# Two-layer MLP after attention on one core: gate and value products rearranged by Strassen's scheme

## Chip, cores and metric

One core of a Trainium2 chip runs the whole program. The metric is device microseconds (us) of one execution, lower is better. The kernel before took 1002.4, 1003.11 and 1007.12 us in three runs (median 1003.11).

## What is computed

From `q`, `k`, `v` (4 batches, 8 heads, 576 positions, 64 wide) an attention output is the sum of a pooled part (means over 4 positions, softmax, repeated) and a local part (each position sees those less than 4 away). With heads side by side it gives 2304 tokens of 512 values, and two MLPs follow, all in float32:

```
x = x.reshape(2304, 512)
h = x @ moe_w_in                      # 512 x 2048
x = (h - tanh(h)) @ moe_w_out         # 2048 x 512
gate = 1 / (1 + exp(-(x @ moe2_w_gate)))   # 512 x 1536
val = x @ moe2_w_val                  # 512 x 1536
out = (gate * val) @ moe2_w_out       # 1536 x 512
```

## The kernel before

Activations are kept transposed: 128 features in the partitions, tokens along the row. Tokens come in six chunks of N = 384. To get float32 accuracy out of TensorE, every operand is held as a high and a low half in the type float32r, and each product of two 128-wide blocks is three matmuls, high by high, high by low, low by high (`mm3`, L228 to L231). A split costs one ScalarE copy (L239, which writes the high half) and one VectorE subtraction (L224, or L242 where the two are staged apart).

**Stage one** (attention and first MLP). Chunk by chunk the loop runs over 16 column blocks f: `do_h` multiplies a chunk by one 512 x 128 block of `w_in` (12 matmuls into one PSUM bank of the tag ab), ScalarE takes tanh (L554), VectorE subtracts, the result is split to `g`; two blocks later `do_y` multiplies g by a 128 x 512 block of `w_out` (12 matmuls, three into each of four banks acc0 to acc3, which hold the sum over all f). The 16 units of first-layer weights stay in SBUF from chunk 0 on, 14 in the pool `wpa` and 2 in `wpb`. Attention for later chunks is woven in between. At a chunk's end `y_out` (L588) copies the four banks out and stores them to DRAM (`y1`); the last chunk is split straight from PSUM.

**Time in the program is counted in ticks**: each `do_h` and each `do_y` calls `tick` twice, so a tick stands for six matmuls of TensorE, and `defer` and `chain` place VectorE, ScalarE and DMA work so many ticks later. From chunk 1 on ScalarE, VectorE, GpSimd and the DMA queue of SyncE (SP) run in exactly the order in which the program issues their work (`in_order`, L602), so an instruction that waits holds up all behind it on its engine.

**Weights** arrive as 1 MB units of packed 64-bit words (`w_load`, L154). A unit is turned into float32 and split by L170 (ScalarE), L176 and L178 (VectorE), L239 (ScalarE) and L193 (VectorE). Units of the second MLP follow when attention is done and its SBUF is given back (`work`, L678), into slots that the last chunk's first-layer weights leave.

**Stage two** (second MLP). The chunks go in pairs; for each pair the loop runs over 12 column blocks f and the two chunks s. Each step multiplies a chunk by one block of `w_gate` (12 matmuls of 384 columns), ScalarE takes the sigmoid from PSUM (L781), then 12 matmuls for the value, VectorE multiplies (L785), the product is split, and `do_out` of the step before adds g times a block of `w_out` to three banks (9 matmuls of 512 columns). There are 72 steps. At f = 11 the banks are copied out and stored (L765, L757):

```
        gate = a_bank()
        h_mm(weight(2, f, 0), key, gate)
        nc.scalar.activation(out=p, in_=gate[:, :N], func=ACTF.Sigmoid)
        tick()
        val = a_bank()
        h_mm(weight(2, f, 1), key, val)
        nc.vector.tensor_tensor(out=p, in0=val[:, :N], in1=p, op=ALU.mult)
        split(g, p)
```

## Time and profile before

| | us |
|---|---|
| three runs | 1002.4, 1003.11, 1007.12 (median 1003.11) |
| profiled execution, first to last instruction | 998.4 |
| around that span, to the median of the runs | 4.7 |
| TensorE busy (matmul) | 979.2, 98% of the span |
| VectorE busy | 419.2, 42% |
| ScalarE busy | 372.2, 37% |
| GpSimd busy | 78.5, 8% |
| TensorE in the chain that ended last | 91% of the span |

The device time of the profiled execution itself is not listed apart from the three runs, so its span is set against their median. Matmuls are pipelined: a row gives some 0.34 us for a matmul of 384 columns, while the next one starts 0.17 us later. Costs of TensorE are therefore read as spacings between starts, not as durations. On VectorE and ScalarE, too, a queued instruction starts some 0.1 us before the row of the one ahead ends.

### The profile page before, as it was taken

How to read it: one execution, taken by the hardware profiler on the slowest of the kernel's cores; microseconds unless marked ns; L12 is line 12 of the kernel's file. 1: busy time of each engine (PE TensorE's matmuls, PEld its weight loads, DVE VectorE, ACT ScalarE, POOL GpSimd, SP SyncE). 2: the span in 40 equal slices, each digit the busy share in tenths (PEclk: the TensorE clock that was granted, in tenths of full speed). 3: DMA queues.
4: the chain of work that ended last, by engine and by line, in shares of the span. 5: the costliest groups of instructions: out<-in, count | busy, mean ns of one | idle time of the engine just before them, and what ended most of it. 6: DMA issues, size and time to landing. Idle time of an engine off the chain costs nothing.

```text
span 998.4 us, 15616 instructions
## 1 busy us (share of the span) xinstructions
PE 979.2 (98%) x6476; PEld 914.6 (92%) x6476; DVE 419.2 (42%) x736; ACT 372.2 (37%) x952; POOL 78.5 (8%) x89
## 2 busy tenths in 40 slices
PE   7889999999999999999999999999999999999998
PEld 7678889999999889999999999999999999999997
DVE  6898864334334343435666553113211114211112
ACT  5867754344344444434456342113111113111111
POOL 2153220300300320000000000000000000000000
PEclk9899999999999999999999999999999999999999
DMA  8566532212203211104444330002000002000001
GB/s 281 165 216 230 177 113 84 62 40 86 61 9 116 63 61 55 60 1 166 159 142 143 127 127 1 9 16 72 32 1 1 3 22 72 32 1 1 1 1 64
DMA packets 33256, 76.63 MB, mean 77 GB/s; under 512 B 3280, under 2 KB 23456, under 8 KB 28832
## 3 DMA queue, kind: packets, MB, share of 16 engines
q1 hardware_dynamic: 33184, 75.62, 23.0%
q8 instruction: 51, 0.84, 0.3%
q14 instruction: 21, 0.17, 0.1%
HBM read 63.02 MB, written 12.58 MB: 76 GB/s over the span
## 4 chain that ended last, share of the span: by engine, by line
PE 91%; DVE 3%; POOL 2%; DMA 2%; ACT 2%; issue 1%; SPq 0%; POOLq 0%; DVEq 0%; ACTq 0%
PE ab L229 18%; PE ab L231 18%; PE ab L230 18%; PE acc L229 10%; PE acc L230 9%; PE acc L231 9%; PE ab L440 2%; PE ab L372 2%; PE ab L305 1%; PE ab L432 1%; PE ab L346 1%; PE ab L334 1%; DMA qk<-in_qk 1%; DVE w L193 1%; PE acc L653 1%
## 5 line engine op out<-in xcount | busy, mean ns | idle before, releaser
L229 PE MATMUL ab<-x,w 128*128 128x384 f32 x952 | 325.5, 342 | 0.3 <-DVE t L242 0.3
L231 PE MATMUL ab<-x,w 128*128 128x384 f32 x952 | 320.4, 337 | 0.0
L230 PE MATMUL ab<-x,w 128*128 128x384 f32 x952 | 320.1, 336 | 0.0
L229 PEld LDWEIGHTS ab<-x,w 128*128 128x128 f32 x952 | 179.2, 188 | 7.6 <-issue 1.8
L230 PEld LDWEIGHTS ab<-x,w 128*128 128x128 f32 x952 | 179.4, 188 | 3.4
L231 PEld LDWEIGHTS ab<-x,w 128*128 128x128 f32 x952 | 179.2, 188 | 0.0
L785 DVE TENSOR_TENSOR p<-ab,p 128x384 f32<-128x384 f32 x72 | 40.2, 558 | 273.4 <-PE ab L231 273.4
L229 PE MATMUL acc<-g,w 128*128 128x384 f32 x384 | 133.2, 349 | 0.0
L230 PE MATMUL acc<-g,w 128*128 128x384 f32 x384 | 129.7, 338 | 0.0
L231 PE MATMUL acc<-g,w 128*128 128x384 f32 x384 | 129.1, 336 | 0.0
L242 DVE TENSOR_TENSOR t<-ab,t 128x384 f32<-128x384 f32 x94 | 52.3, 556 | 153.4 <-ACT t L554 153.4
L781 ACT ACTIVATE p<-ab 128x384 f32<-128x384 f32 x72 | 35.4, 491 | 183.4 <-PE ab L231 183.4
L554 ACT ACTIVATE t<-ab 128x384 f32<-128x384 f32 x94 | 45.9, 488 | 146.3 <-PE ab L231 130.5
L239 ACT ACTIVATE g<-p 128x384 fp32r<-128x384 f32 x72 | 37.8, 524 | 158.0 <-DVE p L785 158.0
L229 PEld LDWEIGHTS acc<-g,w 128*128 128x128 f32 x384 | 72.1, 188 | 2.4 <-issue 1.8
L230 PEld LDWEIGHTS acc<-g,w 128*128 128x128 f32 x384 | 72.3, 188 | 0.7 <-issue 0.6
L231 PEld LDWEIGHTS acc<-g,w 128*128 128x128 f32 x384 | 72.2, 188 | 0.0
L242 DVE TENSOR_TENSOR g<-t,g 128x384 fp32r<-128x384 f32 x96 | 55.9, 583 | 36.6 <-ACT g L239 35.4
L239 ACT ACTIVATE g<-t 128x384 fp32r<-128x384 f32 x96 | 50.3, 524 | 44.7 <-DVE t L242 44.7
L224 DVE TENSOR_TENSOR g<-p,g 128x384 fp32r<-128x384 f32 x72 | 40.2, 559 | 42.6 <-ACT g L239 42.6
L231 PE MATMUL acc<-w,g 128*128 128x512 f32 x144 | 57.1, 396 | 0.0
L230 PE MATMUL acc<-w,g 128*128 128x512 f32 x144 | 57.0, 396 | 0.0
(101 smaller groups left out, 1099.5 us busy)
## 6 DMA issues: line engine op xcount, KB each, us to landing
raw<-in_w SPq DMA_DIRECT2D x34, 1024.0 KB
qk<-in_qk SPq DMA_DIRECT2D x16, 576.0 KB
vr<-in_vp SPq DMA_DIRECT2D x16, 288.0 KB
x<-xo SPq DMA_DIRECT2D x20, 192.0 KB
xs<-x SPq DMA_DIRECT2D x20, 192.0 KB
y<-y SPq DMA_DIRECT2D x20, 192.0 KB
xs<-y SPq DMA_DIRECT2D x20, 192.0 KB
out<-o SPq DMA_DIRECT2D x12, 256.0 KB
```

The costliest lines, as they stand in the source:

```text
L193: nc.vector.tensor_tensor(out=t[:, 1, :], in0=w32, in1=t[:, 0, :].bitcast(F32), op=ALU.subtract)
L224: nc.vector.tensor_tensor(out=dst[:, 1, :], in0=src, in1=dst[:, 0, :].bitcast(F32), op=ALU.subtract)
L229: nc.tensor.matmul(out=o, lhsT=wh, rhs=xh, start=first, stop=False)
L230: nc.tensor.matmul(out=o, lhsT=wh, rhs=xl, start=False, stop=False)
L231: nc.tensor.matmul(out=o, lhsT=wl, rhs=xh, start=False, stop=last)
L239: nc.scalar.activation(out=dst, in_=src, func=ACTF.Copy)
L242: nc.vector.tensor_tensor(out=dst, in0=a, in1=b, op=ALU.subtract)
L372: nc.tensor.matmul(out=sb[r0:r0 + 64, x, :], lhsT=t[r0:r0 + 64, 0, QB * j:QB * j + QB], rhs=t[r0:r0 + 64, 1, w0:w0 + WIN], start=True, sto ...
L440: nc.tensor.matmul(out=ob[r0:r0 + 64, QB * x:QB * x + QB], lhsT=vw[0][:, j - n, i, r0:r0 + 64], rhs=pt[:, x, r0:r0 + 64], start=True, stop ...
L554: nc.scalar.activation(out=t, in_=hb[:, :N], func=ACTF.Tanh)
L781: nc.scalar.activation(out=p, in_=gate[:, :N], func=ACTF.Sigmoid)
L785: nc.vector.tensor_tensor(out=p, in0=val[:, :N], in1=p, op=ALU.mult)
```

## The change

Stage two is taken apart into a gate-and-value stage and an output stage.

The gate-and-value stage works on a pair of column blocks (j, six of them), a pair of token chunks (p, three) and a side (0 gate, 1 value). The 512 inputs are two halves of two 128-blocks (k and k + 2), so weights and tokens form 2 x 2 blocks, and Strassen's scheme (in the Winograd form) gives the four results from seven products in place of eight. The list `PRODUCTS` names for each the weight form, the token form and the bank. A product is six matmuls (two k, three each); the last three are added onto banks that already hold one of the first four, after that one has been read. `ends_of` is what ScalarE and VectorE do after each product; side 0 uses the four ab banks, side 1 the four acc banks. The results of gate times value go to DRAM (`ud`).

Loops: j outermost, then p, then side. So all token forms (42 tiles: three pairs, two k, seven roles) must be in SBUF at once; they take the space of the first layer's weights as the last chunk finishes with it (`x_room`, `room_free`). Weight forms have one tile per side, refilled for each j. Both are made by three generators (`second_weights` for each side, `forms_of_x`) that run as lanes: after every tick `lanes_step` lets them issue work worth `rate` credits; the numbers that they yield are charged. GpSimd forms the token differences.

The output stage then reads the products back chunk by chunk (`u_load`, four steps ahead), splits them (`u_split`, two steps ahead) and runs the same 72 `do_out` steps back to back, with output weights in slots that the token forms of the first pairs have left. TensorE is issued in program order too from the gate stage on. The last chunk of the first MLP goes through DRAM like the others. First-layer weights are allocated two units to a block. On the host, gate and value weights are put into the order of the 2 x 2 blocks.

The diff, cut to what the prediction speaks of (removed lines of stage two are those quoted above and the loop around them):

```diff
-PAIRS = [(0, LAST), (1, 2), (3, 4)]
+PAIRS = [(0, 1), (2, 3), (4, 5)]
 
 WU = 1024
-U1, U2 = F1, F2 * 3 * 512 // WU
+U1 = F1
+NJ = F2 // 2
+
+A11, A12, A22, S1, S2, S3, S4 = range(7)
+B11, B21, B22, T1, T2, T3, T4 = range(7)
+PRODUCTS = [(A11, B11, 0), (S1, T1, 1), (S3, T3, 2), (A12, B21, 3), (S2, T2, 0), (S4, B22, 1), (A22, T4, 2)]
...
-    n_a, n_b, n_c = 14, 2, 2
-    wpa = pool("wpa", n_a, side="right")
+    n_a, n_b = 14, 2
+    wpa = pool("wpa", n_a // 2, side="right")
...
-    y1 = [dram.tile([128, KD, N], F32, name=f"y_{c}") for c in range(LAST)]
+    y1 = [dram.tile([128, KD, N], F32, name=f"y_{c}") for c in range(NC)]
+    ud = [dram.tile([128, F2, 2, N], F32, name=f"u_{p}") for p in range(len(PAIRS))]
...
+    lanes, credit, rate = [], [0.0], [0.0]
+
+    def lanes_step():
+
+        credit[0] = min(credit[0] + rate[0], 1.5)
+        busy = True
+        while lanes and credit[0] > 0 and busy:
+            busy = False
+            for lane in list(lanes):
+                if lane[1] is not None and not lane[1]():
+                    continue
+                lane[1] = None
+                got = next(lane[0], None)
+                if got is None:
+                    lanes.remove(lane)
+                elif callable(got):
+                    lane[1] = got
+                else:
+                    credit[0] -= got
+                busy = True
+                if credit[0] <= 0:
+                    break
+
+    def lane(g):
+        lanes.append([g, None])
+
+    def after(n):
+        at = now[0] + n
+        return lambda: now[0] >= at
...
-        if c == LAST:
-            x_split1(acc[c][e][:, :N], (2, c), e)
-            return
...
+        if c == LAST:
+            defer(1, stored.add, e)
...
-        if "c" not in wpools and not any(x_left[1:]):
+        if "f" not in wpools and not any(x_left[1:]):
             p1.close()
-            wpools["c"] = pool("wpc", n_c, reuse_waits="tile")
+            wpools["f"] = pool("wpf", 1, reuse_waits="tile")
             wpools["raw2"] = pool("raw2", 1, reuse_waits="tile")
-            wpools["xp2"] = pool("xp2", KD, reuse_waits="tile")
-            w_load(U1 + 2)
+            wpools["xs"] = pool("xs2", 3, reuse_waits="tile")
+            lane(second_weights(0))
+            lane(second_weights(1))
+            lane(forms_of_x())
+            rate[0] = 0.6
...
+    def second_weights(side):
+
+        while len(wt) < U1:
+            yield after(1)
+        for j in range(NJ):
+            raw = raw_load(side, 2 * j + side)
+            yield after(6)
+            yield from to_f32(raw)
+            w, t = (x.bitcast(F32).rearrange("p (b c) -> p b c", b=4) for x in words_of(raw))
+            for o, a, b, op in (
+                (0, w[:, 0], w[:, 3], ALU.add), (2, w[:, 1], w[:, 0], ALU.subtract),
+                (1, t[:, 0], w[:, 1], ALU.subtract), (3, w[:, 2], t[:, 1], ALU.subtract),
+            ):
+                nc.vector.tensor_tensor(out=t[:, o], in0=a, in1=b, op=op)
+                yield 0.45
+            yield lambda: j == 0 or (j - 1, side) in made
+            f = wpools["f"].tile([128, 2, 7, 256], F32R, tag=f"f{side}", name="f")
+            parts = ((w[:, 1:4], slice(0, 3)), (t, slice(3, 7)))
+            for src, at in parts:
+                copy(f[:, 0, at], src)
+                yield 0.0
+            for src, at in parts:
+                nc.vector.tensor_tensor(out=f[:, 1, at], in0=src, in1=f[:, 0, at].bitcast(F32), op=ALU.subtract)
+                yield 1.1
+            form[j, side] = f
+        for i in range(side, NJ, 2):
+            raw = raw_load(side, 2 * NJ + i)
+            yield after(6)
+            yield from to_f32(raw)
+            yield lambda: (NJ - 1, 1, i // 4) in made
+            w32 = words_of(raw)[0].bitcast(F32)
+            t = out_slot(i)
+            copy(t[:, 0, :], w32)
+            yield 0.0
+            nc.vector.tensor_tensor(out=t[:, 1, :], in0=w32, in1=t[:, 0, :].bitcast(F32), op=ALU.subtract)
+            yield 1.3
+            wo[i] = t
...
+            if k < n_a // 2 + 1:
+                t = block(wpa if k < n_a // 2 else wpools["b"], "x").rearrange("p a b -> p (a b)")
+                extra.extend(t[:, 768 * i:768 * i + 768].rearrange("p (i n) -> p i n", i=2) for i in range(5))
+            else:
+                extra.append(xp.tile([128, 2, N], F32R, tag="x", name="x"))
...
+        k = n_blocks[0]
+        return (LAST, min(2 * k + 1, F1 - 1)) in y_done
...
+    def forms_of_x():
+
+        for p, (ca, cb) in enumerate(PAIRS):
+            for k in range(2):
+                yield lambda: room_free()
+                if cb == LAST:
+                    yield lambda: k in stored and k + 2 in stored
+                    yield after(1)
+                raw = {}
+                for n, (c, kk) in enumerate(((cb, k + 2), (cb, k), (ca, k), (ca, k + 2))):
+                    raw[c, kk] = (wpools["xs"] if n < 2 else xs).tile([128, N], F32, tag="xs", name="xs")
+                    nc.sync.dma_start(out=raw[c, kk], in_=y1[c][:, kk, :])
+                b11, b12, b21, b22 = raw[ca, k], raw[cb, k], raw[ca, k + 2], raw[cb, k + 2]
+                t2 = wpools["xs"].tile([128, N], F32, tag="xs", name="t2")
+                t3 = xs.tile([128, N], F32, tag="xs", name="t3")
+                yield after(5)
+
+                def sub(out, a, b):
+                    nc.gpsimd.tensor_tensor(out=out, in0=a, in1=b, op=ALU.subtract)
+
+                sub(t3, b22, b12)
+                sub(b12, b12, b11)
+                sub(t2, b22, b12)
+                todo = [(B11, b11), (B22, b22), (B21, b21), (T3, t3), (T1, b12), (T2, t2), (T4, b21)]
+                prev = None
...
+                    copy(t[:, 0, :], src)
+                    if prev:
+                        nc.vector.tensor_tensor(
+                            out=prev[0][:, 1, :], in0=prev[1], in1=prev[0][:, 0, :].bitcast(F32), op=ALU.subtract
+                        )
+                    if role == T3:
+                        sub(b21, b21, t2)
+                    prev = (t, src)
+                    yield 0.6
...
+    in_order(E.PE, E.SP, E.Activation, E.DVE, E.Pool)
...
+    def ends_of(j, side, p):
+
+        bank = [t[:, :N] for t in banks_of(side)]
+        room = gp if side else xp
+        c = [room.tile([128, 2, N], F32R, tag="g" if side else "x", name="c").bitcast(F32) for _ in range(2)]
+        one = xs.tile([128, N], F32, tag="xs", name="one")
+        two = xs.tile([128, N], F32, tag="xs", name="two")
+
+        def done(i):
+            if not side:
+                nc.scalar.activation(out=c[i], in_=c[i], func=ACTF.Sigmoid)
+                gates[i] = c[i]
+            else:
+                nc.vector.tensor_tensor(out=c[i], in0=c[i], in1=gates[i], op=ALU.mult)
+                defer(1, store, ud[p][:, 2 * j + i], c[i])
+
+        three = xs.tile([128, N], F32, tag="xs", name="three")
+
+        yield bank
+        yield lambda: copy(one, bank[0])
+        yield lambda: copy(two, bank[1])
+        yield lambda: add(two, bank[2], two)
+        yield lambda: add(c[0][:, 0, :], bank[3], one)
+        yield lambda: (copy(three, bank[0]), add(c[1][:, 1, :], bank[0], two))
+        yield lambda: (add(c[0][:, 1, :], bank[1], three), defer(1, done, 0))
+        yield lambda: (add(c[1][:, 0, :], bank[2], three), defer(1, done, 1))
+
+    for j in range(NJ):
+        for p in range(len(PAIRS)):
+            for side in range(2):
+                while (j, side) not in form or p not in formed:
+                    rate[0] = 0.9
+                    tick()
+                rate[0] = 0.4 if side else 0.65
+                w = form[j, side]
+                ends = ends_of(j, side, p)
+                bank = next(ends)
+                for n, (a, b, at) in enumerate(PRODUCTS):
+                    for k in range(2):
+                        x = xform[p, k, b]
+                        wh, wl = (w[:, i, a, 128 * k:128 * k + 128] for i in range(2))
+                        mm3(
+                            bank[at], wh, wl, x[:, 0, :], x[:, 1, :], n < 4 and k == 0,
+                            k == 1, skip_group_check=n > 3,
+                        )
+                    defer(1, next(ends))
+                    tick()
+                if p == len(PAIRS) - 1:
+                    made.add((j, side))
+                made.add((j, side, p))
...
+    def u_load(p, f, s):
+        us[p, f, s] = xs.tile([128, N], F32, tag="xs", name="u")
+        nc.sync.dma_start(out=us[p, f, s], in_=ud[p][:, f, s, :])
+
+    def u_split(p, f, s):
+        n = len(gs2_made)
+        room = (gp, xp, xp, gp, gp)[n % 5]
+        gs2_made.append(n)
+        g = gs2[p, f, s] = room.tile([128, 2, N], F32R, tag="x" if room is xp else "g", name="g")
+        split(g, us.pop((p, f, s)))
...
+    for n in range(4):
+        u_load(*steps[n])
+    for n in range(2):
+        u_split(*steps[n])
+    rate[0] = 0.9
+    for n, step in enumerate(steps):
+        if n + 4 < len(steps):
+            u_load(*steps[n + 4])
+        do_out(*step, gs2.pop(step))
...
+        if n + 2 < len(steps):
+            u_split(*steps[n + 2])
```

## Rows read from the trace of the kernel before

**Rows 1.** busy time of each engine by stretch (DVE is VectorE, ACT ScalarE):

```profile
core 0: us, PE busy (x) PEld busy (x) DVE busy (x) ACT busy (x) POOL busy (x), PEclk, DMA share, GB/s
110.00:476.00 366.00, 363.58 (x2810) 341.73 (x2810) 161.03 (x325) 158.15 (x482) 45.15 (x54) 1.00 0.24 73
476.00:542.50 66.50, 66.50 (x386) 66.50 (x385) 45.15 (x65) 34.88 (x56) 0.00 (x0) 1.00 0.47 162
542.50:993.40 450.90, 450.90 (x2379) 421.84 (x2377) 120.38 (x199) 101.46 (x185) 0.00 (x0) 1.00 0.09 30
```

**Rows 2.** groups of instructions by line, stage two alone (542.5 to 993.4 us):

```profile
L231 PE MATMUL ab<-x,w 128*128 128x384 f32 x576 | 193.7, 336 | 0.0
...
L231 PE MATMUL acc<-w,g 128*128 128x512 f32 x144 | 57.1, 396 | 0.0
...
L231 PE MATMUL ab<-w,g 128*128 128x512 f32 x72 | 28.4, 395 | 0.0
```

**Rows 3.** TensorE's timeline: start us, duration, line, tiles:

```profile
540.73 0.34 PE L229 MATMUL acc<-g,w 128*128 128x384 f32 x1
...
542.81 0.35 PE L229 MATMUL ab<-x,w 128*128 128x384 f32 x1
...
978.99 0.34 PE L229 MATMUL ab<-x,w 128*128 128x384 f32 x1
...
983.15 0.39 PE L229 MATMUL acc<-w,g 128*128 128x512 f32 x1
...
985.25 0.34 PE L229 MATMUL ab<-x,w 128*128 128x384 f32 x1
```

**Rows 4.** groups of VectorE and ScalarE by line, whole span:

```profile
L785 DVE TENSOR_TENSOR p<-ab,p 128x384 f32<-128x384 f32 x72 | 40.2, 558 | 273.4 <-PE ab L231 273.4
...
L178 DVE SCALAR_TENSOR_TENSOR raw<-raw 128x1024 int32<-128x1024 int32 x34 | 42.1, 1239 | 2.4 <-ACT raw L170 0.9
...
L170 ACT ACTIVATE raw<-raw 128x1024 f32<-128x1024 f32 x34 | 39.2, 1152 | 0.7 <-DMA raw<-in_w 0.7
L239 ACT ACTIVATE w<-raw 128x1024 fp32r<-128x1024 f32 x34 | 38.8, 1140 | 14.5 <-DVE raw L178 14.5
L239 ACT ACTIVATE g<-p 128x384 fp32r<-128x384 f32 x72 | 37.8, 524 | 158.0 <-DVE p L785 158.0
L781 ACT ACTIVATE p<-ab 128x384 f32<-128x384 f32 x72 | 35.4, 491 | 183.4 <-PE ab L231 183.4
```

**Rows 5.** VectorE's timeline where its queue is full:

```profile
471.24 0.69 DVE L176 TENSOR_SCALAR raw<-raw 128x1024 int32<-128x1024 int32 x1
471.85 0.55 DVE L242 TENSOR_TENSOR t<-ab,t 128x384 f32<-128x384 f32 x1
472.31 1.22 DVE L178 SCALAR_TENSOR_TENSOR raw<-raw 128x1024 int32<-128x1024 int32 x1
473.44 0.55 DVE L242 TENSOR_TENSOR g<-t,g 128x384 fp32r<-128x384 f32 x1
```

**Rows 6.** ScalarE's timeline where its queue is full:

```profile
547.86 0.53 ACT L239 ACTIVATE g<-p 128x384 fp32r<-128x384 f32 x1 [1.48 <-DVE p L785]
548.29 1.12 ACT L239 ACTIVATE w<-raw 128x1024 fp32r<-128x1024 f32 x1
549.31 0.48 ACT L781 ACTIVATE p<-ab 128x384 f32<-128x384 f32 x1
```

**Rows 7.** GpSimd's timeline, startup, then VectorE's in the same stretch:

```profile
66.79 0.73 POOL L283 TENSOR_TENSOR vd<-vd,vr 72x256 f32<-72x256 f32 x1
...
68.60 1.87 POOL L276 TENSOR_TENSOR m<-m,qk 128x288 f32<-128x288 f32 x1
...
69.60 1.43 DVE L176 TENSOR_SCALAR raw<-raw 128x1024 int32<-128x1024 int32 x1
...
77.25 0.69 DVE L176 TENSOR_SCALAR raw<-raw 128x1024 int32<-128x1024 int32 x1
```

More of the change, by code (lines that the diff above doesn't have):

```diff
@@ L131, in raw_pool @@
     def raw_pool(i):
[L132 to L136 removed]
+        return raw1 if i < n_a and i % (n_b + 1) != n_b else rawp
     def slot_pool(i):
@@ L182, in w_high @@
     def w_high(i):
-        if i > ready[0] or not slot_free(i):
+        if i > ready[0]:
             defer(1, w_high, i)
@@ L187, in w_high @@
         w32 = words(i)[0].bitcast(F32)
[L188 removed]
+        t = slot(i)
         copy(t[:, 0, :], w32)
@@ L691, in work, with raw_load, to_f32 @@
         if now[0] % PACE[c] == PACE[c] - 1:
             w_begin()
-    def x_split_first(k):
-        c = PAIRS[0][0]
-        x_split1(xraw.pop(((2, c), k)), (2, c), k, wpools["xp2"])
+    stored, made = set(), set()
+    form, xform, extra = {}, {}, []
+    def raw_load(side, i):
+        raw = (rawp, wpools["raw2"])[side].tile([128, WU], I64, tag="raw", name="raw")
+        nc.sync.dma_start(out=raw, in_=w2[i])
+        return raw
+    def to_f32(raw):
+        lo, hi = words_of(raw)
+        as_f32 = hi.bitcast(F32)
+        nc.scalar.activation(out=as_f32, in_=as_f32, func=ACTF.Prelu, scale=2.0 ** -112, alpha=2.0 ** 32)
+        nc.vector.tensor_scalar(out=lo, in0=lo, scalar1=29, scalar2=None, op0=ALU.logical_shift_right)
+        yield 0.8
+        yield after(1)
+        nc.vector.scalar_tensor_tensor(
+            out=lo, in0=hi, scalar=3, in1=lo, op0=ALU.logical_shift_left, op1=ALU.bitwise_or
+        )
+        yield 1.25
@@ L727, in tile_kernel, with banks_of, add @@
         do_y(*todo.pop(0))
-    xs2 = pool("xs2", 2, reuse_waits="tile")
-    steps = [(i, f, s) for i in range(len(PAIRS)) for f in range(F2) for s in range(2)]
-    banks, ends = {}, []
-    def out_banks(i, s):
+    beat[0] = None
+    in_order(E.PE, E.SP, E.Activation, E.DVE, E.Pool)
+    def banks_of(side):
+        if side:
+            return [acc_bank(t) for t in range(4)]
+        return [ps.tile([128, 512], F32, tag="ab", bufs=4, name="ab") for _ in range(4)]
+    def add(out, a, b):
+        nc.vector.tensor_tensor(out=out, in0=a, in1=b, op=ALU.add)
@@ new lines, in tile_kernel @@
+    steps = [(p, f, s) for p in range(len(PAIRS)) for f in range(F2) for s in range(2)]
+    us, gs2, banks, last_rooms = {}, {}, {}, []
+    def u_load(p, f, s):
[7 more added lines that the diff above has]
+        split(g, us.pop((p, f, s)))
@@ L735, in out_banks, with result, do_out @@
         return [acc_bank(3)] + [ps.tile([128, 512], F32, tag="ab", bufs=4, name="ab") for _ in range(2)]
-    def do_out(i, f, s, g):
-        w = weight(2, f, 2)
+    def result():
+        if not last_rooms:
+            t = block(wpa, "o").bitcast(F32).rearrange("p a b -> p (a b)")
+            last_rooms.extend(t[:, DM * i:DM * i + DM] for i in range(8))
+        return last_rooms.pop(0)
+    def do_out(p, f, s, g):
+        while f // 2 not in wo:
+            tick()
+        w = wo[f // 2][:, :, 512 * (f % 2):512 * (f % 2) + 512]
         if f == 0:
-            banks[s] = out_banks(i, s)
+            banks[s] = out_banks(s)
         for t, bank in enumerate(banks[s]):
@@ L744, in do_out @@
             if f == F2 - 1:
-                row = PAIRS[i][s] * N + t * 128
-                last = i == len(PAIRS) - 1
-                if last:
-                    if not ends:
-                        ends.extend(p.tile([128, WU], I64, tag="raw", name="ends").bitcast(F32) for p in (rawp, wpools["raw2"]))
-                    at = 3 * s + t
-                    o = ends[at // 4][:, at % 4 * DM:at % 4 * DM + DM]
-                else:
-                    o = xs2.tile([128, DM], F32, tag="o", name="o")
-                if last and s == 1 and t == 2:
+                row = PAIRS[p][s] * N + t * 128
+                o = result()
+                if p == len(PAIRS) - 1 and s == 1 and t == 2:
                     half = DM // 2
```

138 lines of the change are left out of this document (69 added, 69 removed).

## The prediction, made before the changed kernel ran

> **What bounds the kernel now.** I read the stretches first [rows 1], to see which engine is full where. From 110 us on TensorE is busy all the time: in stage two, 542.5 to 993.4 us, it is busy 450.90 of 450.90 us at a granted clock of 1.00, while VectorE has 120.4 us of work and ScalarE 101.5. Then the groups of stage two [rows 2] say what it does: 3 x 576 = 1728 matmuls of 384 columns and 3 x (144 + 72) = 648 of 512. Last, the timeline [rows 3] gives their price. From 978.99 to 983.15 us lie the 24 matmuls of one gate and value, 0.1733 us each; from 983.15 to 985.25 nine of 512 columns, 0.2333 each. 1728 x 0.1733 + 648 x 0.2333 = 299.5 + 151.2 = 450.7 us, the whole stage. So stage two is a sum of matmuls and nothing else; what takes matmuls away takes time away, as long as VectorE, ScalarE and the transfers keep up.
>
> **Matmuls removed.** A group of old work (two column blocks, two chunks, one side) is 2 x 2 x 4 x 3 = 48 matmuls; by seven products it is 7 x 2 x 3 = 42. There are 6 x 3 x 2 = 36 groups, so 36 x 6 = 216 matmuls fewer: 216 x 0.1733 = **37.4 us**. The new products change bank after six matmuls, the old after twelve. The y matmuls of stage one change after three, and twelve of them take 540.73 to 542.81 us, again 0.1733 each [rows 3]; I take no cost for it. The Trainium skill (TensorE: Matmul & The Clock Gate, "Wait — 56ns, not 53.3ns?") puts a warm matmul at its columns over 2.4 GHz plus about 2.5 ns, 162.5 ns here; by that the gain would be 35.1 us. The rows have 173.3 ns at full clock, and they decide.
>
> **Work added in the gate and value stage.** Prices: VectorE on 384 columns 0.56 us by its row, 1024 columns 1.24 [rows 4]; queued, starts follow each other after 0.46 (384), 1.13 (1024) and 0.61 (the shift) [rows 5]. ScalarE: 384 columns 0.49 to 0.52, 1024 columns 1.14 [rows 4], queued 0.43 and 1.02 [rows 6]. In between, by a straight line, 768 columns are 0.86 (VectorE) and 0.80 (ScalarE) queued, 256 columns 0.36. Per pair of groups (gate, value), which TensorE does in 84 x 0.1733 = 14.56 us: VectorE ten additions and two multiplications of 768, at row durations 10 x 0.56 + 2 x 0.95 = 7.5 us; ScalarE six copies and two sigmoids, 6 x 0.49 + 2 x 0.89 = 4.7. Per column pair j (43.7 us) the weight forms add, for each side, a shift, a merge, four sums of 256 and two splits on VectorE, 2 x 5.9 = 11.8, and 2 x 3.2 = 6.4 on ScalarE. Whole stage, 262 us of TensorE: VectorE 18 x 7.5 + 6 x 11.8 = 206 (79%), ScalarE 18 x 4.7 + 6 x 6.4 = 123 (47%). Neither becomes the bound on average; the question is order.
>
> **Bank returns.** The fifth product adds onto the first one's bank, the sixth onto the second's, the seventh onto the third's, so TensorE waits until ScalarE or VectorE has read it. Each has three products, 3.1 us, for that. Without lane work the copy of 0.5 us is done long before: nothing lost.
>
> **Change of column pair, the tight place.** A side has one weight-form tile. It can be refilled only after the last group of that side, and must be ready one group (7.28 us) later. I queue it, from the end of the gate's last product as 0: ScalarE the second sigmoid (after VectorE's last addition, 0.65) to 1.45, the copy of bank 0 to 1.9, the two form copies (768, 1024) to 3.7, the copy of bank 1 to 4.2; TensorE wants bank 1 at 5.2. VectorE: form subtractions from 2.8 to 5.05, the addition from bank 2 to 5.6; TensorE wants bank 2 at 6.24, and the forms' first low half at 7.3. So nothing is late, by 0.6 us. In the next group, where VectorE carries two multiplications and the other side's forms, the margin comes out the same. Queueing all of it with a tenth added to every duration loses 4.7 us over the stage, with a fifth added 17 us (estimates worked from rows 4 to 6). Bounds 0 to 17, and I take 1.0, near the unstretched rows. Loads of weights wait behind the form's last read, with ScalarE and VectorE queued behind them; ScalarE waited 0.7 us in all for the 34 loads before [rows 4], so nothing is added.
>
> **Token forms.** A tick is six matmuls, 1.04 us. From the end of attention (some 450 us) to the end of stage one at 542.8 are about 89 ticks, worth 89 x 0.6 = 53 credits. Needed by then: two pairs' token forms (each 2 x 9 x 0.6 = 10.8), both weight forms of j = 0 (12.1) and what of j = 1 needs no tile (7.7), 41.4 in all. Space comes as the last chunk frees its weights; the second pair's last block is free 12 ticks before the end, and this pair is wanted only 14 ticks after it. VectorE's share of this is about 30 us of 92 beside its own 27%; in the last chunk before it was 45.15 of 66.50 us busy, and TensorE had no gap [rows 1]. Cost 0. The third pair needs the last chunk through DRAM: store, load, then twice 5 + 10 ticks. It is issued two ticks behind its use, but what comes last is wanted four and six products into the group. Nothing to 2 us; I take 0.5.
>
> **Into the output stage.** Before its first low half is there, VectorE has in its queue the last weights' split (1.14), a multiplication (0.86), the last addition and the split itself (0.48 each), from 0.4 us before TensorE's last product ends: to about 2.8 us after. TensorE has two matmuls (0.47 us) without it. Cost **2.4 us**, bounds 1.0 (nothing of the lane in front) and 4. Its 72 steps of nine matmuls are unchanged, 2.1 us each; a split takes 0.52 us of ScalarE and 0.56 of VectorE a step [rows 4], two steps ahead. The end of the program is the same. First-layer weights in blocks of two, and the new order on the host: no work added, cost 0, plus or minus some 2 us as startup is packed again.
>
> **Sum.** 998.4 - 37.4 + 2.4 + 1.0 + 0.5 = 964.9 us of span. The profiled span lies 4.7 us under the median of the runs (1003.1), and I carry that: **969.6 us**.
>
> **Rivals.**
> 1. VectorE and ScalarE late at column changes. For: margins of 0.6 us in queues that are full there, and nothing in the trace before shows such queues. Against: average loads of 79% and 47%. Losing 8 to 17 us: 977 to 986, say 981. Chance 0.15.
> 2. GpSimd and VectorE in each other's way in the last chunk. GpSimd's differences, 24 in all, 16 of them while stage one still runs, would be some 1.1 us each (256 columns take 0.73). When both are at work both stretch: a GpSimd row of 1.87 us overlaps a VectorE shift of 1.43 that otherwise takes 0.69 [rows 7]. If each of the 16 holds VectorE for 1.1 us and half of that reaches the chain from tanh to the y matmuls, 16 x 0.55 = 9 us go: 978. Against: y comes two blocks later, some 8 us for a chain of four operations. Chance 0.09. The Trainium skill (SBUF — State Buffer, "Who interferes with whom") has the two share a port pair, the loser blocked for the whole instruction; the stretched rows agree.
> 3. Slower than before: TensorE waits for its bank in every group, at the fifth product, because ScalarE's copy of the first bank stands behind other work that waits. The price is per group, 36 times; from 37.4 / 36 = 1.04 us each on the gain is gone; at 1.5 us each it is 54 us lost, about 1020. For: engines in strict order, with sigmoids, form copies and load waits ahead of bank copies. Against: 2.3 us of slack at the fifth product, and only two or three of a column pair's six groups have lane work on ScalarE. Chance 0.05.
> 4. Fewer matmuls, no gain: spacing grows to 1728 / 1512 x 0.1733 = 0.198 us with more changes of bank and weights, 1003. The y matmuls speak against it [rows 3]. Chance 0.03.
>
> **How the numbers follow.** My own case has 0.68. It runs from 965 (nothing lost, less the scatter of the runs) to 976 (upper bounds of the two transitions, a stretched queue at 5 us). Rivals 1 and 2 reach to 986; taking them in, and startup's 2 us below, the range is 963 to 986, which leaves rivals 3 and 4 and the far ends out. A measurement of this kernel can tell some 0.5%, 5 us, from no change. Faster by more than that: 0.68 + 0.15 + 0.09 = 0.92; same 0.03; slower 0.05.
>
> **What would show it.** 1512 matmuls of 384 columns with starts 0.173 us apart; the gate and value stage some 263 us long, the output stage 151 to 154. One gap of about 2.4 us of TensorE between them, ending on a VectorE split. Around each column change at most fractions of a microsecond, waits for bank reads. Wrong if TensorE's gaps in the gate stage add up to over 5 us, if gaps open before 543 us with VectorE's chain late (rival 2), or if each group shows a wait at its fifth product (rival 3).

## The result, and the profile after

The changed kernel takes **974.28 us** (median of four runs, 972.85 to 975.31), the kernel before 1002.75 beside it (four runs, 1001.01 to 1007.12): ratio **0.972**, 95% interval 0.969 to 0.975. Forecast were 969.6 us, 963 to 986, faster with 0.92. The direction held; the time came out 4.7 us above the forecast, inside the range and inside my own case (965 to 976). The profiled span is 973.2 us, 8.3 more than the 964.9 of the sum.

The page of the changed kernel first: the span, and the busy time of each engine in the whole of it.

```profile
span 973.2 us, 15952 instructions
...
PE 950.2 (98%) x6260; PEld 883.3 (91%) x6260; DVE 543.9 (56%) x960; ACT 430.6 (44%) x1056; POOL 103.8 (11%) x113
```

TensorE has 216 matmuls fewer than before and is as full as it was, 98%. VectorE rose from 42% to 56%, ScalarE from 37% to 44%. The stretches, with the columns of [rows 1]: attention and stage one, the last chunk, the gate and value stage, what lies between it and the second step of the output stage, and the rest of that stage.

```profile
core 0: us, PE busy (x) PEld busy (x) DVE busy (x) ACT busy (x) POOL busy (x), PEclk, DMA share, GB/s
110.00:477.00 367.00, 365.49 (x2822) 343.40 (x2821) 165.94 (x339) 159.64 (x497) 45.28 (x54) 1.00 0.24 74
477.00:544.90 67.90, 67.90 (x394) 67.90 (x393) 46.15 (x79) 32.29 (x68) 17.51 (x16) 1.00 0.27 90
544.90:811.80 266.90, 266.90 (x1514) 266.71 (x1512) 189.95 (x309) 122.83 (x197) 8.14 (x8) 1.00 0.32 116
811.80:820.10 8.30, 3.92 (x10) 2.77 (x10) 7.18 (x11) 3.97 (x7) 0.00 (x0) 0.79 0.46 147
820.10:969.40 149.30, 149.27 (x640) 119.31 (x638) 44.30 (x81) 37.20 (x76) 0.00 (x0) 1.00 0.37 116
```

Two things stand out against [rows 1], where stage two was one full stretch. The gate and value stage is full to the last tenth (266.90 of 266.90) and yet 4.9 us longer than 1512 x 0.1733 = 262.0. And a hole has opened between the stages: TensorE is busy for 3.92 of 8.30 us, at a granted clock of 0.79. In the last chunk, where GpSimd's differences now lie beside the chain of stage one (17.51 us of work in 16 of them), TensorE is full.

The first and the last gate matmul, in TensorE's timeline, give the price of one, as [rows 3] did before.

```profile
544.97 0.33 PE L264 MATMUL ab<-x,f 128*128 128x384 f32 x1
...
583.80 0.34 PE L265 MATMUL acc<-x,f 128*128 128x384 f32 x1
...
585.92 0.34 PE L265 MATMUL acc<-x,f 128*128 128x384 f32 x1
...
811.59 0.34 PE L266 MATMUL acc<-x,f 128*128 128x384 f32 x1
```

From 544.97 to 811.59 lie 1511 steps: 266.62 / 1511 = 176.5 ns, and the 12 steps from 583.80 to 585.92 are as long, 177. Before, twelve matmuls of 384 columns took 2.08 us, 173.3 ns each [rows 3]. No gap hides in it: every matmul simply comes 3.1 ns later. 1512 x 3.1 ns = **4.7 us**.

TensorE's waits over the whole span (us in total, times, longest; the first is startup's), and its timeline at the hole:

```profile
PE acc L687 <- DMA id_sb<-in_ident: 5.8, 1, 5.8
...
PE acc L264 <- ACT g L274: 2.5, 1, 2.5
PE acc L266 <- DVE g L259: 1.9, 1, 1.9
```

```profile
814.39 0.50 PE L264 MATMUL acc<-w,g 128*128 128x512 f32 x1 [2.47 <-ACT g L274]
814.73 0.40 PE L265 MATMUL acc<-w,g 128*128 128x512 f32 x1
817.04 0.80 PE L266 MATMUL acc<-w,g 128*128 128x512 f32 x1 [1.91 <-DVE g L259]
...
818.49 0.63 PE L266 MATMUL acc<-w,g 128*128 128x512 f32 x1
818.91 0.63 PE L264 MATMUL acc<-w,g 128*128 128x512 f32 x1
...
820.11 0.39 PE L264 MATMUL acc<-w,g 128*128 128x512 f32 x1
```

The last gate matmul starts at 811.59, so another could start at 811.76. The output stage's first comes 2.63 us after that: it waits for ScalarE's high half of the first split. Its third comes 2.08 us late: it waits for VectorE's low half. The other starts of the first step, most of them 0.43 us apart where 0.2333 is normal, add 1.54 us, 0.10 of it between the first two matmuls. The granted clock from 816.7 to 819.9 is 0.50. Together 8.35 us for nine matmuls that take 2.10: **6.25 us** lost. Who was late, in ScalarE's timeline and then VectorE's:

```profile
807.82 1.19 ACT L742 ACTIVATE raw<-raw 128x1024 f32<-128x1024 f32 x1
811.37 1.17 ACT L742 ACTIVATE raw<-raw 128x1024 f32<-128x1024 f32 x1 [2.36 <-DMA raw<-in_w]
812.42 0.50 ACT L274 ACTIVATE three<-acc 128x384 f32<-128x384 f32 x1
812.79 1.14 ACT L274 ACTIVATE w<-raw 128x1024 fp32r<-128x1024 f32 x1
813.80 1.36 ACT L274 ACTIVATE g<-u 128x384 fp32r<-128x384 f32 x3
```

```profile
811.31 0.69 DVE L743 TENSOR_SCALAR raw<-raw 128x1024 int32<-128x1024 int32 x1 [0.58 <-DMA raw<-in_w]
812.95 0.56 DVE L905 TENSOR_TENSOR c<-acc,two 128x384 f32<-128x384 f32 x1 [0.95 <-ACT three L274]
813.43 0.55 DVE L905 TENSOR_TENSOR c<-acc,three 128x384 f32<-128x384 f32 x1
813.96 1.23 DVE L785 TENSOR_TENSOR w<-raw,w 128x1024 fp32r<-128x1024 f32 x1
815.11 0.95 DVE L922 TENSOR_TENSOR c<-c 128x768 f32<-128x768 f32 x1
815.97 0.55 DVE L905 TENSOR_TENSOR c<-acc,three 128x384 f32<-128x384 f32 x1
816.44 1.01 DVE L259 TENSOR_TENSOR g<-u,g 128x384 fp32r<-128x384 f32 x2
```

ScalarE stands for 2.36 us at a load of output weights that are wanted much later. Behind it in the queue is the copy of the last group's bank (812.42), behind that the weights' high half, and only then the split that TensorE waits for. VectorE's last additions wait for that copy, and its own split (816.44) comes behind the weights' low half.

The 8.3 us over the sum: the gate stage starts at 544.97 instead of 542.81, +2.2; it lasts 266.8 instead of 263.5 (262.0 and the 1.5 I had allowed), +3.3; the hole is 6.25 instead of 2.4, +3.85; from the last matmul to the end 4.2 instead of 5.0, -0.8. These add up to 0.25 too much, by rounding. The -0.8 lies behind the last copy, in the last stores (3.8 us before, 3.0 now); no run looks into it.

### The profile page after: what moved, and what is told of

The parts are those of the page before. It is cut to its first block, busy times and chain, and to the rows that moved or that the text cites. A ratio compares the mean times of both kernels' runs of the same rounds, so it can differ in the third digit from the quotient of the medians.

```text
span 973.2 us, 15952 instructions
## 1 busy us (share of the span) xinstructions
PE 950.2 (98%) x6260; PEld 883.3 (91%) x6260; DVE 543.9 (56%) x960; ACT 430.6 (44%) x1056; POOL 103.8 (11%) x113
## 5 line engine op out<-in xcount | busy, mean ns | idle before, releaser
L264 PE MATMUL ab<-x,w 128*128 128x384 f32 x376 | 132.5, 352 | 0.5 <-DVE t L277 0.5
L265 PE MATMUL ab<-x,w 128*128 128x384 f32 x376 | 127.2, 338 | 0.0
L266 PE MATMUL ab<-x,w 128*128 128x384 f32 x376 | 127.1, 338 | 0.0
L266 PE MATMUL ab<-x,f 128*128 128x384 f32 x252 | 85.2, 338 | 0.0
L266 PE MATMUL acc<-x,f 128*128 128x384 f32 x252 | 85.2, 338 | 0.0
L265 PE MATMUL ab<-x,f 128*128 128x384 f32 x252 | 85.2, 338 | 0.0
L265 PE MATMUL acc<-x,f 128*128 128x384 f32 x252 | 85.2, 338 | 0.0
L264 PE MATMUL ab<-x,f 128*128 128x384 f32 x252 | 85.1, 338 | 0.0
L264 PE MATMUL acc<-x,f 128*128 128x384 f32 x252 | 85.0, 338 | 0.0
L259 DVE TENSOR_TENSOR g<-u,g 128x384 fp32r<-128x384 f32 x72 | 37.6, 555 | 78.4 <-ACT g L274 78.3
L264 PEld LDWEIGHTS ab<-x,w 128*128 128x128 f32 x376 | 71.2, 189 | 4.8 <-issue 2.0
L265 PEld LDWEIGHTS ab<-x,w 128*128 128x128 f32 x376 | 71.4, 190 | 0.1
L266 PEld LDWEIGHTS ab<-x,w 128*128 128x128 f32 x376 | 71.2, 189 | 0.0
```

The lines of the kernel that those rows point to most:

```text
L259: nc.vector.tensor_tensor(out=dst[:, 1, :], in0=src, in1=dst[:, 0, :].bitcast(F32), op=ALU.subtract)
L264: nc.tensor.matmul(out=o, lhsT=wh, rhs=xh, start=first, stop=False, **kw)
L265: nc.tensor.matmul(out=o, lhsT=wh, rhs=xl, start=False, stop=False, **kw)
L266: nc.tensor.matmul(out=o, lhsT=wl, rhs=xh, start=False, stop=last, **kw)
```

## The experiments

Two costs were to be explained, the hole and the 176.5 ns. "Lost between the stages" below is the time from the last gate matmul to the last output matmul over what 648 of them take unbroken (151.14 us, with the step to the first); it is 6.2 us in the changed kernel.

**e1, nothing of the lane work in the last group.**

```diff
                 rate[0] = 0.4 if side else 0.65
+                if (j, p, side) == (NJ - 1, len(PAIRS) - 1, 1):
+                    rate[0] = credit[0] = 0.0
```

> The lanes issue nothing during the last group of gate and value; what is left of the output weights is made in the output stage. The two loads in flight stay where they are. In the changed kernel 8.35 us pass from the end of the gate stage to the start of the second output step, where nine matmuls take 2.1: 6.25 us lost. Theory (ScalarE and VectorE stood behind the loads of the last two units, and the copies and splits behind them): loss 0.5 to 2.5 us, no stretch at the lower clock, 969 to 971 us in all. Rival (the read-back of the gated values, or the change of stage itself, is late): loss stays above 5 us, 974.

968.21 us (967.0 to 969.74), ratio to the kernel before 0.9655 [0.9601, 0.9708], a little under the 969 to 971 expected; span 967.7, lost between the stages 1.3 us, spacing 176.5 as in the changed kernel. TensorE's timeline of this kernel at the same place, then the window 812 to 821 of it, then that of the changed kernel:

```profile
811.01 0.34 PE L266 MATMUL acc<-x,f 128*128 128x384 f32 x1
811.35 0.50 PE L264 MATMUL acc<-w,g 128*128 128x512 f32 x1
811.69 0.40 PE L265 MATMUL acc<-w,g 128*128 128x512 f32 x1
812.87 0.50 PE L266 MATMUL acc<-w,g 128*128 128x512 f32 x1 [0.78 <-DVE g L259]
```

```profile
812.00:821.00 9.00, 8.22 (x36) 6.60 (x36) 9.00 (x13) 6.71 (x10) 0.00 (x0) 1.00 0.64 207
```

```profile
812.00:821.00 9.00, 4.70 (x13) 3.52 (x14) 7.31 (x12) 4.67 (x9) 0.00 (x0) 0.81 0.50 152
```

The first split no longer waits, the second half waits 0.78 us, and the clock stays at 1.00. The reading of the two gated chunks from DRAM is the same in both, so it is not what made the hole. The hole is the lane work's place in the queues.

**e2, without the last two units of output weights.** The third and the fourth unit are used twice instead, in the place of the last two.

```diff
-        for i in range(side, NJ, 2):
+        for i in range(side, NJ - 2, 2):
...
+    wo[4], wo[5] = wo[2], wo[3]
```

> Leaves out the last two of six units of output weights (their load, conversion and split); blocks 8 to 11 are multiplied by the weights of blocks 4 to 7 in their place. Theory (queue behind late loads): loss between the stages 0.5 to 2.5 us in place of 6.25, as with the lanes paused. Rival 1 (the bytes of the loads slow the read-back, the queue does not matter): loss small here but unchanged with the lanes paused. Rival 2 (read-back late by itself): above 5 us here too.

970.03 us (one run), span 968.2, lost between the stages 1.3, as in e1. e1 moves the same loads and splits a little later and loses no more than e2, which leaves them out: it is not their bytes or their work that costs, but that they stand ahead of the last group's copies.

**e3, other operands by column pair.** Pairs 1 to 5 multiply something else: 1 and 3 take their tokens from another tile, 2 and 3 their weights, 4 and 5 use one half of an operand twice.

```diff
+                        if j in (1, 3):
+                            x = xform[2, 1, T4]
+                        if j in (2, 3):
+                            wh, wl = (xform[0, 0, B11][:, i, 128 * k:128 * k + 128] for i in range(2))
...
+                        if j == 4:
+                            wl = wh
+                        if j == 5:
+                            xl = xh
```

> The gate stage's matmuls start 176.5 ns apart on average, those of stage one 173.3: some 4.7 us over 1512. Operands are changed by column pair, the rest stays: pair 0 as it is; pair 1 takes all moving operands from one token form in the pool that stage one used for x; pair 2 all stationary ones from a token form in the first block; pair 3 both; pair 4 uses the high half of the weights for the low one; pair 5 the high half of the tokens for the low one. So these pairs compute something else. Theory A (the place of the moving operand, in the blocks): 173.3 ns in pairs 1 and 3, 176.5 in the others. Theory B (the place of the stationary operand, the weight-form tile): 173.3 in pairs 2 and 3. Theory C (the order of banks and accumulation, or the way of issue): 176.5 in all.

972.97 us (one run), span 970.9. The spacing by column pair, worked out from TensorE's timeline (here of all the kernels that touch it, mean ns between starts without the gaps):

```
column pair           0      1      2      3      4      5
changed kernel      176.5  176.5  176.5  176.5  176.5  176.5
e3                  176.5  173.4  173.5  173.3  176.5  176.5
e7                  176.5  175.9  173.3  176.1  173.4  174.5
e8                  173.4  173.3  173.3  173.3  173.3  173.4
e10                 176.5  174.5  176.3  175.0  174.5  176.1
e5 (behind a gap)   176.5  174.8  174.3  175.3  175.0  174.5
```

Either operand from elsewhere gives the old spacing back, where theories A and B each had only one of the two; which half is used does not matter. The products, their order and their banks are the same in all six pairs, so the change of bank after six matmuls costs nothing, as predicted. What is left is where the operands lie, or that in pairs 1 to 3 one of them stays the same from product to product; e7 and e8 decide between the two.

**e4, an eighth product.** The fourth product is added twice in each group: 216 matmuls more, as many as before.

```diff
-                    for k in range(2):
+                    for k in (0, 1, 0, 1)[:4 if n == 3 else 2]:
```

> The fourth product of each group is computed twice, the second time over the first, so eight products are done for seven: 36 x 6 = 216 matmuls more. Theory (the gate stage lasts as long as its matmuls): 216 x 0.1765 = 38.1 us more, about 1012 us. Rival (VectorE and ScalarE set the pace in part, so added matmuls fill waits): less than 34 us more.

1006.77 us (one run), span 1004.7. The gate stage goes from 540.60 to 845.55, 304.95 us where the changed kernel has 266.8: 38.1 us for 216 x 176.5 ns = 38.1. So the stage as it stands lasts as long as its matmuls. The span grows by less, 31.5, because this execution starts the stage 4.4 us earlier and loses 2.3 less behind it. By the span alone the rival's "less than 34 us" would hold; the stage itself decides against it.

**e5, more work for VectorE.** Two of a group's five additions are made twice over, into the same place.

```diff
-        yield lambda: add(c[0][:, 0, :], bank[3], one)
+        yield lambda: [add(c[0][:, 0, :], bank[3], one) for _ in range(2)]
...
-        yield lambda: (add(c[1][:, 0, :], bank[2], three), defer(1, done, 1))
+        yield lambda: ([add(c[1][:, 0, :], bank[2], three) for _ in range(2)], defer(1, done, 1))
```

> Two additions of each group of gate and value are done twice with the same result, 72 more VectorE instructions of 384 columns, some 0.5 us each when queued, 36 us of VectorE in a stage of 267. Theory (VectorE has room in the gate stage): the stage stays at 266.8 us, no gap of TensorE in it over 0.5 us. Rival (margins at a change of column pair are used up): gaps of TensorE at the five changes, 5 to 17 us more.

980.59 us (one run), span 978.6; the gate stage takes 276.1 us, 9.3 more. I held that VectorE had room for it; that is a miss. TensorE's waits in this kernel:

```profile
PE acc L264 <- ACT one L274: 5.2, 5, 1.2
...
PE ab L264 <- DVE two L905: 2.1, 2, 1.2
```

In column pairs 1 to 4 TensorE loses 1.7 to 1.8 us each, nearly all of it in one gap at the fifth product of the second group behind the column change. In the last pair it loses 4.3 us, of which 0.8 there. That makes 11.4 us in all, and part of it comes back in a shorter spacing behind the gaps (table). One gap behind a column change, in TensorE's and in ScalarE's timeline:

```profile
598.08 0.44 PE L264 MATMUL acc<-x,f 128*128 128x384 f32 x1 [1.20 <-ACT one L274]
```

```profile
595.08 0.85 ACT L919 ACTIVATE c<-c 128x768 f32<-128x768 f32 x1 [4.04 <-DVE c L905]
596.80 0.84 ACT L919 ACTIVATE c<-c 128x768 f32<-128x768 f32 x1 [0.88 <-DVE c L905]
597.55 0.47 ACT L274 ACTIVATE one<-acc 128x384 f32<-128x384 f32 x1
```

The copy of the first bank stands behind two sigmoids that wait for VectorE's additions. The other 3.5 us of the last pair are another thing: there the lanes make output weights, and VectorE's addition from a bank stands behind their splits, or behind a conversion that waits for their load (2.72 us idle before it at 798.00). VectorE's timeline at one of these gaps; the matmul that needs the bank starts at 791.19:

```profile
788.32 2.35 DVE L785 TENSOR_TENSOR w<-raw,w 128x1024 fp32r<-128x1024 f32 x2
790.59 0.55 DVE L905 TENSOR_TENSOR two<-ab,two 128x384 f32<-128x384 f32 x1
```

On average VectorE still has 51 of 276 us free. So rival 1's mechanism is real and close: two additions a group, 1.1 us, are enough to start it, and a third of what they cost comes from the lane work that also made the hole.

**e6, the pause and an earlier first split.** Besides the pause of e1, the first two gated blocks are read back at the start of the last group and the first split is made after its fourth product.

```diff
+                            if n == 3:
+                                u_split(*steps[0])
```

> Lanes paused in the last group as in the run with the pause, and the first two read-backs and the first split are issued within the last group of the gate stage. Theory (with the pause, what is left of the loss is VectorE's last addition and the split behind it): loss between the stages below 0.5 us where 1.32 remained, some 1 us less than the kernel with the pause alone. Rival (the remaining 1.3 us belong to the change of stage): 1.3 us again.

970.46 us (969.33 to 976.93), ratio 0.9715 [0.9677, 0.9753]; span 968.0, lost between the stages 2.1, more than e1. TensorE's wait:

```profile
PE acc L264 <- DVE c L905: 1.6, 2, 1.3
```

With the split ready, the output stage's first step waits for its banks: VectorE has still to add from them. A miss, and a new wait in place of the old one.

**e7, weight forms at other addresses.** The weight-form tile is made longer and starts 0, 64, 128, 32, 192 and 256 bytes further in column pairs 0 to 5.

```diff
+            at = (0, 16, 32, 8, 48, 64)[j]
+            f = f[:, at:at + 2 * 7 * 256].rearrange("p (i a c) -> p i a c", i=2, a=7)
```

> The weight-form tiles are 256 bytes longer and the forms start, by column pair, 0, 64, 128, 32, 192 and 256 bytes into them; nothing else changes. Stationary addresses are then 32, 96, 32, 64, 96, 32 modulo 128 bytes, with nearly all moving operands at 96. In stage one moving ones are at 32 and stationary at 96. Theory D (the pair of addresses modulo 128 decides, and 96 moving with 32 stationary is the slow pair): 173.4 ns in pairs 1 and 4, 176.5 in pairs 0, 2 and 5; pair 3 open. Theory E (an operand that stays the same from matmul to matmul made the pairs fast in the run with swapped operands): 176.5 ns in all pairs.

973.18 us (one run), span 971.2. Nothing but the offset differs, and the spacing moves (table): 173.3 at 128 bytes, 173.4 at 192, 176.5 at 0, between them at 64, 32 and 256. Theory E, 176.5 in all pairs, is out, and theory D too: it had pair 1 fast and pair 2 slow. So addresses matter, but not by the offset modulo 128 bytes alone, since 0, 128 and 256 differ. Each pair here is also entered from another offset; e10 asks what that does.

**e8, token forms 64 bytes further.**

```diff
-                extra.extend(t[:, 768 * i:768 * i + 768].rearrange("p (i n) -> p i n", i=2) for i in range(5))
+                extra.extend(t[:, 768 * i + 16:768 * i + 784].rearrange("p (i n) -> p i n", i=2) for i in range(5))
```

> The token forms start 64 bytes further into their blocks; nothing else changes. Moving operands of the gate stage are then at 32 modulo 128 bytes, as the stationary ones. Theory D (addresses modulo 128): 173.4 ns throughout the gate stage, 1512 x 3.1 ns = 4.7 us less. Theory E (operands that stay the same): 176.5 as before.

967.41 us (one run), span 965.3. The first and the last gate matmul, and the stage as a window, of this kernel:

```profile
540.87 0.35 PE L264 MATMUL ab<-x,f 128*128 128x384 f32 x1
...
803.12 0.34 PE L266 MATMUL acc<-x,f 128*128 128x384 f32 x1
```

```profile
541.00:803.30 262.30, 262.26 (x1513) 261.73 (x1511) 189.03 (x309) 121.84 (x197) 8.12 (x8) 1.00 0.32 118
```

262.25 us from first to last, 4.4 less than the 266.62 of the changed kernel, with the same work on every engine. At 173.3 ns the stage would take 4.7 us less; 0.3 of it goes into one new gap in the last column pair. So the shift takes back the whole of the spacing's cost. The span fell by 7.9, but 4.1 of that is the earlier start of the stage (540.87), which the edit does not touch.

**e9, all that had seemed to help.** The pause and the early split of e6, with the first output step on the other set of banks, and the shift of e8.

```diff
-        if s == 0:
+        if s:
...
-        return [acc_bank(3)] + [ps.tile([128, 512], F32, tag="ab", bufs=4, name="ab") for _ in range(2)]
+        return [ps.tile([128, 512], F32, tag="ab", bufs=4, name="ab") for _ in range(3)]
```

> Three mendings together: lanes paused in the last group with the first read-backs and the first split issued early, token forms 64 bytes further, and the output stage's first step on the ab banks in place of the acc banks that VectorE is still reading (the run with the early split waited 1.6 us there). Theory: spacing 173.4 ns (4.4 us less than in the changed kernel), loss between the stages below 0.6 us (5.7 less): some 10 us less than the changed kernel, 962 to 966 us. Rival (the loss only moves to another wait, on banks or slots of the output stage): 967 or more.

963.22 us (962.01 to 967.21), ratio 0.9633 [0.961, 0.9656]. The gate stage has 173.3 ns, but between the stages 2.7 us are lost, more than in e1 and a miss against the 0.6 expected: the bank is free, the splits are late instead. That the time still lies in the 962 to 966 expected is luck: this execution starts the stage at 541.11 us, 3.9 earlier than the changed kernel's.

```profile
804.45 0.50 PE L264 MATMUL ab<-w,g 128*128 128x512 f32 x1 [0.95 <-ACT g L274]
...
807.90 0.50 PE L266 MATMUL acc<-w,g 128*128 128x512 f32 x1 [0.49 <-DVE g L259]
...
810.45 0.50 PE L266 MATMUL ab<-w,g 128*128 128x512 f32 x1 [0.18 <-DVE g L259]
```

**e10, the same addresses, another entry.** At the head of column pairs 1 to 5 stands one more matmul of 64, 128, 192, 256 or 320 columns, into a bank that the first product then overwrites.

```diff
+                cols = (0, 64, 128, 192, 256, 320)[j]
+                if cols and p == side == 0:
+                    nc.tensor.matmul(
+                        out=bank[0][:, :cols], lhsT=w[:, 0, A11, 0:128], rhs=xform[p, 0, B11][:, 0, :cols],
+                        start=True, stop=True,
+                    )
```

> At the head of column pairs 1 to 5 TensorE gets one more matmul, of 64, 128, 192, 256 and 320 columns, on a bank that is then overwritten; all addresses are those of the changed kernel. Theory F (the spacing is a pattern that depends on how a stretch is entered): some pairs at 173.3 ns. Theory G (the two operands' addresses alone decide): 176.5 ns in all pairs.

972.71 us (one run), span 970.9. With every address as in the changed kernel, pairs 1 and 4 drop to 174.5, pair 3 to 175.0; pairs 2 and 5 hardly move (table). So the address alone does not decide either: how the stream stands when it enters a stretch counts too. e5 says the same, where a gap comes ahead of the stretch.

**The changed kernel again**, beside the last of these, for the scatter of its profile:

> The changed kernel once more, beside the mended one on the same chip: 972.5 to 975.5 us; loss between the stages near 6 us, spacing 176.5 ns.

974.28 us (973.41 to 976.99), ratio 0.9743 [0.9723, 0.9762]; span 974.8, gate stage from 546.04 to 812.66 at 176.5 ns, 6.8 us lost between the stages. Both costs come back; the start of the stage has now lain anywhere from 540.6 to 546.0 in kernels whose work up to there is the same.

**e11, the pause and the shift alone.** The edits of e1 and e8 together.

> The pause of e1 and the shift of the token forms by 64 bytes of e8, without the early split and the exchange of banks of e9. In e9 TensorE lost 2.7 us from the last gate matmul to the last output matmul against an unbroken run (1.35 up to the second step and 1.35 behind it, in waits for the splits of steps two and three), in e1 1.3 us in all. Theory (early split and exchanged banks only move the wait, and put VectorE's and ScalarE's splits behind): 1.3 to 1.5 us lost here, gate stage 262.2 us at 173.3 ns, so from the first gate matmul to the last output matmul 262.2 + 151.0 + 1.4 = 414.6 us, where e9 took 415.9 and the changed kernel 424.0. Rival (the pause alone needs the slower matmuls as cover, and with 173.3 ns the first split is later against TensorE): 2.5 us or more lost here, 415.7 or more. The start of the gate stage has lain between 540.6 and 546.0 us, so the time itself may be 961 to 967 us by either.

964.17 us (963.45 to 965.55, five runs), ratio 0.964 [0.9615, 0.9665]. From the first gate matmul to the last output matmul 543.43 to 958.16, 414.7 us: the first reading held, 1.3 us lost between the stages, 1.2 us less over this stretch than e9 (541.11 to 957.00, 415.9). In the median of the runs the two can't be told apart. Either beats both kernels, the changed one by some 10 us.

## Why the prediction was right, and where it was not

**Right, and shown: matmuls removed.** The step had 216 matmuls fewer and a stage that lasts as long as its matmuls. e4 puts them back and gets 38.1 us for them, 176.5 ns each, to the tenth.

**Failed: "I take no cost for it", on the spacing.** The step read 173.3 ns off rows of the kernel before, on other tiles, and asked only about banks. The banks are not the reason (e3 and e8 keep them and get 173.3 to 173.5). But the operands of the new products lie in new tiles, and at these addresses the stream runs at 176.5: +4.7 us, which the 1.5 us for column changes and for the third pair's token forms, both not needed, cut to +3.3. Rival 4 had longer spacing, at 198 ns, 25 ns more; it came at an eighth of that, and not from the changes of bank and weights that the rival named. No row of before could tell that a spacing belongs to the place of its operands: there all of these matmuls had 173.3.

**Failed: "Cost 2.4 us" into the output stage.** Its bounds were 1.0 and 4, measured are 6.25. I queued VectorE's work and left ScalarE out (TensorE's first wait, 2.47 us, ends on ScalarE's split), and I had written of the loads that "nothing is added", from 0.7 us of waiting in 34 loads [rows 4]. Those rows are an engine with room. Here one load had ScalarE stand for 2.36 us with the last group's copy behind it, and behind TensorE's two gaps the clock was down, some 1.4 us more. With the lane held back (e1) the loss is 1.3, near the lower bound that I had set for just that case.

**Within its bounds: change of column pair.** I took 1.0 us with margins of 0.6; measured is no gap at all. VectorE had 190 us of work where I had 206. The longer spacing is not what gave it time: at 173.3 ns (e8, e11) no column change has a gap either. The 0.3 us that these two lose in the stage come 35 us after the last change, at the seventh product of the fifth group of the last pair: in e8 the matmul at 794.86 needs the bank of an addition that stands behind a split of output weights, in VectorE's queue.

```profile
793.12 1.22 DVE L785 TENSOR_TENSOR w<-raw,w 128x1024 fp32r<-128x1024 f32 x1
794.26 0.55 DVE L905 TENSOR_TENSOR two<-ab,two 128x384 f32<-128x384 f32 x1
```

I had looked for this kind of wait behind weight forms and not behind output weights. e5 shows how near the edge is: 1.1 us a group more, and TensorE stands for 11.4 us. The chance of 0.15 was not too high.

```profile
L922 DVE TENSOR_TENSOR c<-c 128x768 f32<-128x768 f32 x34 | 32.5, 957 | 0.9
L919 ACT ACTIVATE c<-c 128x768 f32<-128x768 f32 x36 | 30.2, 845 | 30.6 <-DVE c L905 30.6
```

These groups of the gate stage (mean ns behind the comma; 957 and 845) are the two prices on 768 columns that I had drawn by a straight line: 0.95 and 0.89 were used. That line was not drawn exactly: through the rows it gives 0.97 for VectorE's row, 0.78 for ScalarE's queued 768 columns where I had 0.80, and 0.31 to 0.33 for 256 columns where I had 0.36. None of it changes the sum.

**Right: bank returns, token forms, GpSimd.** No wait for a bank shows in the gate stage (rival 3), and no gap in the last chunk (rival 2): TensorE is 67.90 of 67.90 us busy while GpSimd makes 16 differences in 17.51 us, 1.09 each as estimated. The output stage, too, runs at 0.2333 us a matmul behind its first step: 149.27 of 149.30 us busy.

**Within its bound: startup.** "Plus or minus some 2 us" was +2.2 at the start of the gate stage. Kernels that are the same up to there start it from 540.6 to 546.0 us, so most of it is scatter of one execution against another. The scatter goes with the granted clock of the first 110 us: 0.92 in the changed kernel and its repeat (start at 545.0 and 546.0 us), 0.94 in e1, e3, e6, e7 and e11 (543.4 to 544.4), 0.97 in e4, e5 and e8 (540.6 to 540.9). (e2, e9 and e10 have a second low stretch, near 325 us.) Why the clock is lower for longer in some executions is not shown. The kernel before has 0.94 and 542.8, 0.6 to 1.6 us earlier than kernels of the same clock, so a part may belong to the change; one execution of it can't tell.

**Carried, and not there: 4.7 us around the span.** That was a span from one execution against the median of others. In the changed kernel the profiled execution took 975.31 us for a span of 973.2, and the median lies 1.1 above the span. By luck the 3.6 us too much here hid as much of the 8.3 us missing in the sum; what is left is the error of 4.7.

## What to carry to other kernels

An engine with half its time free still makes others late when a load that isn't due stands ahead of work that is: before a change of stage, stop feeding the queues with work for later. Averages say nothing of the margin; a doubled instruction does, in one run. And a spacing between matmuls read off one pair of tiles is good for that pair: where TensorE is full, try the new tiles at another offset.

## What the runs showed of the hardware that was not expected

Back-to-back matmuls of 384 columns at full granted clock start 173.3 or 176.5 ns apart, or at a value between, by the addresses of their operands in SBUF (tokens 64 bytes further: 3.1 ns less for each of 1512 matmuls, e8) and by what the stream did on entry (e10). The rule behind it stays open: e7 excludes that the offset modulo 128 bytes alone decides, e10 that addresses alone do.

After two gaps of 2.47 and 1.91 us with two matmuls between them TensorE ran at half its clock (granted 0.50 from 816.7 to 819.9), 0.43 us between starts of 512 columns, which is 512 columns at 1.2 GHz, until 820.11; with one gap of 0.78 us (e1) it stayed at full clock. The Trainium skill (TensorE: Matmul & The Clock Gate, "Back-to-back issue gap") gives some 131 ns per matmul of 512 columns for a stream of weight loads and matmuls. No run here agrees: with its float32r operands the output stage has 233.3 in every one.
